# Decode attention with a gated MLP on one core: 16 instead of 24 rows of the output projection take the wide path, in steps of 4, and their sums are added earlier

## Chip, cores and metric

One core of one Trainium2 chip. The metric is the device time of one execution in microseconds (us). A "span" is the length of an execution inside the profile. It is shorter than the timed value of the same execution by 1.3 to 1.5 us in most executions and by 1.7 to 2.0 us in some, so that a time can be 0.5 us longer for a reason that lies outside the span.

In the profile PE is TensorE (its matmuls), PEld its loading of weights, PEq its sequencer, ACT ScalarE, DVE VectorE, POOL GpSimd and SP SyncE, which issues the loads. "Landing" is the signal that a load is complete. In a chain of waits, "issue" is time in which the engine waited for nothing that the profile shows. L716 is line 716 of the kernel.

## The reference, cut to what matters

```python
# one query token, 32 heads, 16384 cached keys and values, Dh = 128, D = 512
q = (x @ wq).reshape(1, 1, 32, 128).transpose(0, 2, 1, 3)
p = softmax(einsum('bhqd,bhkd->bhqk', q, k_cache) * Dh ** -0.5)
o = einsum('bhqk,bhkd->bhqd', p, v_cache)
a = o.transpose(0, 2, 1, 3).reshape(1, 1, 4096) @ wo        # wo: 4096 x 512, 4 MB
b = gated_mlp(x)                                            # small, done at the start
return g * a + (1 - g) * b
```

The caches are 2 x 128 MB, and every byte is read once. `wo` is the last thing read.

Of the kernel before, what the change touches and what calls it, by code (L numbers as in the profile page):

```python
# [31 lines left out]
NS = Dh // W  # L32
NG = KP // 4
TG = 8
WG = 8
NT = NG // TG
ZB = F // 4
K_CUTS = (0, 128, 256)
V_CUTS = (0, 160, 224, 256)
WO_CUTS = (0, 16, 24, 28, 31, 32)  # L40
WIDE = 24
inv_sqrt_dh = float(Dh) ** -0.5


# [39 lines left out]
def take(eng, sem, n=1):  # L84

    eng.wait_ge(sem, n).then_inc(sem, -n)  # L86


def matmul_again(nc, eng, out, lhsT, rhs, **flags):

    ins = eng.matmul(out, lhsT=lhsT, rhs=rhs, **flags).ins  # L91
    again = dataclasses.replace(ins, ldweights=False)
    todo = nc.cur_bb.bb.instructions
    assert todo[-1].name == ins.name
    todo[-1] = again
    return bass.BassInstruction(again)


def matmul_at(nc, eng, bank, col, shape, lhsT, rhs, static, again=False):


    m, n = shape
    flags = dict(start=False, stop=False, skip_group_check=True)
    with nc.discard():
        like = eng.matmul(bank[col:col + m, 0:n], lhsT=static[0], rhs=static[1], **flags).ins
    ins = eng.matmul(bank[0:m, 0:n], lhsT=lhsT, rhs=rhs, **flags).ins  # L106
    assert like.tile_size == ins.tile_size and like.tile_position == (0, col)
    moved = dataclasses.replace(ins, outs=like.outs, tile_position=like.tile_position,
                                ldweights=False if again else ins.ldweights)
    todo = nc.cur_bb.bb.instructions  # L110
    assert todo[-1].name == ins.name
    todo[-1] = moved
    return bass.BassInstruction(moved)


def matmul_on(nc, eng, emit, at, known={}):


    todo = nc.cur_bb.bb.instructions
    n = len(todo)  # L120
    ins = emit().ins
    new = list(todo[n:])
    assert new[-1].name == ins.name
    moving = [a for a in ins.ins if isinstance(a, mybir.RegisterAccessPattern)]
    assert len(moving) == len(at)
    ends = {a.regref: r for a, r in zip(moving, at)}
    set_here = {x.outs[0].regref for x in new[:-1]}
    for name in set(ends) - set_here:
        assert known[name] == ends.pop(name)
    live = {a.regref for a in ins.outs if isinstance(a, mybir.RegisterAccessPattern)}  # L130
    keep = [new[-1]]
    for x in reversed(new[:-1]):
        name = x.outs[0].regref
        if name in ends:
            reg, off = known[name] = ends.pop(name)
            assert isinstance(x, mybir.InstRegisterAlu) and x.op == ALU.add
            src, imm = x.ins
            imm = dataclasses.replace(imm, value=imm.value + off)
            x = dataclasses.replace(x, ins=(dataclasses.replace(src, regref=reg.name), imm))
        elif name in live:  # L140
            live |= {a.regref for a in x.ins if isinstance(a, mybir.RegisterAccess)}
        else:
            continue
        keep.append(x)
    assert not ends
    todo[n:] = keep[::-1]
    return bass.BassInstruction(new[-1])


def registers_first(nc, n, then=None):  # L150

    todo = nc.cur_bb.bb.instructions
    new = list(todo[n:])
    todo[n:] = [i for i in new if isinstance(i, mybir.InstRegisterAlu)]
    if then is not None:
        then()
    for i in new:
        if not isinstance(i, mybir.InstRegisterAlu):
            todo.append(i)
# [17 lines left out]
def gated_mix_kernel(nc, A_x, A_k_cache, A_v_cache, A_wq, A_wo, B_x, B_w_in, B_w_sp, B_b_sp,  # L177
# [83 lines left out]
    def counter(e, name, value):  # L261
        reg = e.alloc_register(name)
        e.reg_mov(reg, value)
        return reg
# [205 lines left out]
    def warm(e, n):  # L470
        for j in range(n):
            args = (m_ps[0], ident[:, :], zero[:, :])
            flags = dict(start=True, stop=True, skip_group_check=True)
            if j:
                matmul_again(nc, e, *args, **flags)
            else:
                e.matmul(args[0], lhsT=args[1], rhs=args[2], **flags)

    def fill(e, m, n=1):
        for _ in range(n):  # L480
            matmul_again(nc, e, m_ps[0][96:96 + m, :], ident[:, 0:m], zero[:, :], start=True,
                         stop=True, skip_group_check=True)
# [163 lines left out]
    def hand(e, loaded, to, n):  # L646
        e.wait_ge(loaded, 16).then_inc(to, n)
        e.nop().then_inc(loaded, -16)
# [34 lines left out]
    def pool_wo(e):  # L683
        e.wait_ge(*d_zero)
        e.wait_ge(*o2_ok)
        for j, (a, b) in enumerate(zip(WO_CUTS[:-1], WO_CUTS[1:])):
            if a < WIDE:
                hand(e, ld_o[j], wo_s, (min(b, WIDE) - a) // WG)

    pool.raw(pool_wo)  # L690

    def pe_wide(e):
        va, pa = (counter(e, n, 0) for n in ("wa", "oa"))
        warm(e, 2)
        with e.Fori(0, WIDE // WG) as t:
            w8 = wo[:, bass.ds(t * (WG * D), WG * D)]
            o8 = o2[:, bass.ds(t * WG, WG)]
            n = len(nc.cur_bb.bb.instructions)
            for j in range(WG):
                ins = matmul_on(nc, e, lambda: matmul_at(  # L700
                    nc, e, d_ps, 32 * (j % 4), (1, D), o8[:, j:j + 1], w8[:, j * D:(j + 1) * D],
                    (o2[:, 0:1], wo[:, 0:D])), [(va, in_wo + 2 * j * D), (pa, 2 * j)])
            registers_first(nc, n, lambda: take(e, wo_s))
            ins.then_inc(pe.sem, 1)
            fill(e, 1)
            e.reg_alu(va, va, 2 * WG * D, ALU.add)
            e.reg_alu(pa, pa, 2 * WG, ALU.add)

    pe.raw(pe_wide)
    pe.n += WIDE // WG  # L710
    w_ok = act.op(lambda e: e.copy(out=d_sb[:, :], in_=d_ps), wait=[(pe.sem, pe.n)], mark=True)


    def add(lhsT, rhs, wait, mark=False):
        for s in range(NC):
            ok = pe.op(lambda e, s=s: e.matmul(  # L716
                a_ps[32 * s:32 * s + 1, 0:DQ], lhsT=lhsT, rhs=rhs[:, s * DQ:(s + 1) * DQ],
                start=False, stop=False, skip_group_check=True), wait=wait if s == 0 else (),
                mark=mark and s == NC - 1, inc=(half, 1) if mark and s == 0 else None)
        return ok  # L720

    for j, (a, b) in enumerate(zip(WO_CUTS[:-1], WO_CUTS[1:])):
        for k in range(max(a, WIDE), b):
            y_ok = add(o2[:, k:k + 1], wo[:, k * D:(k + 1) * D],
                       [(ld_o[j], 16)] if k == a else (), k == H - 1)
        if b == 28:
            add(ones_f[:, 0:1], d_sb[:, :], [w_ok])
    for q in (dve, act):
        mine = range(NC)[:NC // 2] if q is dve else range(NC)[NC // 2:]
# [27 lines left out]
def build(inputs):  # L757
    import numpy as _np
    import concourse.bacc as _bacc
    from concourse import mybir as _mybir  # L760

    nc = _bacc.Bacc("TRN2", target_bir_lowering=False, num_devices=1, dynamic_dma_scratch_size=4096)
    arrays, args = {}, []
    for name in _INS:
        a = _np.ascontiguousarray(inputs[name])
        if a.dtype.kind in "iu":
            a = a.astype(_np.int64)
        arrays[f"in_{name}_dram"] = a
        args.append(nc.dram_tensor(f"in_{name}_dram", a.shape, _mybir.dt.from_np(a.dtype), kind="ExternalInput").ap())
    for i, (shape, dtype) in enumerate(_OUTS):  # L770
        dt = _mybir.dt.from_np(_np.dtype(dtype))
        args.append(nc.dram_tensor(f"out_{i}_dram", shape, dt, kind="ExternalOutput").ap())
    gated_mix_kernel(nc, *args)
    return nc, arrays
# [9 lines left out]
```

## The kernel before: what the change and the argument touch

Each of the 128 partitions holds 32 of the 4096 rows of `wo`; row k means the k-th of them, a 128 x 512 slice. The load of `wo` is split into five pieces, which land one after another (at 643.12, 645.61, 646.88, 647.87 and 648.15 us). The vector `o2` (128 x 32) holds the attention output, one column for each row.

A row can be multiplied in two ways. The *wide* way is one matmul of 512 columns into one of four strips of 32 array columns, so that four rows run side by side (in the first step below their matmuls start at 643.334 to 643.344 us and take 0.38 us each); it leaves four partial sums in the PSUM bank `d_ps`, which ACT copies to `d_sb` and a matmul with ones adds into `a_ps`. The *direct* way is two matmuls of 256 columns, in two strips, straight into `a_ps`.

```python
WG = 8                               # wide rows in one loop step
WO_CUTS = (0, 16, 24, 28, 31, 32)    # pieces of the load of wo, in rows
WIDE = 24                            # rows 0-23 go the wide way

def pool_wo(e):                      # POOL passes "piece has landed" on to PE, one unit for each step
    e.wait_ge(*d_zero); e.wait_ge(*o2_ok)
    for j, (a, b) in enumerate(zip(WO_CUTS[:-1], WO_CUTS[1:])):
        if a < WIDE:
            hand(e, ld_o[j], wo_s, (min(b, WIDE) - a) // WG)

def pe_wide(e):
    warm(e, 2)                       # matmuls on zeros, while PE waits
    with e.Fori(0, WIDE // WG) as t:
        ...                          # WG matmuls of 512 columns into strips j % 4 of d_ps;
        registers_first(nc, n, lambda: take(e, wo_s))     # before them, take one unit
        ins.then_inc(pe.sem, 1)
        fill(e, 1)                   # one matmul on zeros
        ...
w_ok = act.op(lambda e: e.copy(out=d_sb[:, :], in_=d_ps), wait=[(pe.sem, pe.n)], mark=True)

for j, (a, b) in enumerate(zip(WO_CUTS[:-1], WO_CUTS[1:])):
    for k in range(max(a, WIDE), b): # direct rows; the first of a piece waits for its landing
        y_ok = add(o2[:, k:k + 1], wo[:, k * D:(k + 1) * D],
                   [(ld_o[j], 16)] if k == a else (), k == H - 1)
    if b == 28:                      # the wide part's sums: between rows 27 and 28
        add(ones_f[:, 0:1], d_sb[:, :], [w_ok])
# then half of a_ps is copied to res by DVE, half by ACT (L731), and SP stores res
```

The softmax here doesn't subtract the row's maximum and nothing guards it: scores larger than these inputs give would overflow.

## Time and profile before

| | before |
|---|---|
| time, median of the first 3 runs | 651.94 us (651.72 to 652.34) |
| span of the profiled run | 650.2 us |
| bytes read, mean rate | 279.58 MB, 430 GB/s |
| PE busy, DVE busy | 65%, 52% |

From the page of the kernel before (part 1: busy us, share and count of instructions; part 2: busy tenths in 40 equal slices of the span):

```profile
span 650.2 us, 7735 instructions
...
PE 423.0 (65%) x2464; PEld 44.4 (7%) x1304; DVE 336.0 (52%) x159; ACT 45.8 (7%) x112; POOL 2.1 (0%) x10
...
PEclk9959788969779696987969798686978968798999
DMA  9999989999999999999999989999999999999898
...
HBM read 279.58 MB, written 0.00 MB: 430 GB/s over the span
```

The DMA engines are full from end to end (8 or 9 tenths busy in every slice), and no compute engine is (PE, the busiest, 65%). PEclk is the granted PE clock in tenths; it moves between slices (5 to 9 tenths), and it is high in the last ones (9 tenths in the last three).

The chain of waits of the kernel before, its last pieces (start us, us, what):

```profile
619.38 27.50 DMA bufs<-in_A_wo_dram
646.88 0.04 issue
646.92 1.64 PE ps_all L716 x20
648.56 0.02 issue
648.58 0.41 DVE res L731
```

The execution ends on the load of `wo`, the direct matmuls (L716) and one copy. The timeline of the same tail (start us, us, engine, line, operation, count, and in brackets the idle time before it and what ended it; L106 on `o` are the wide rows, L91 the filler, L716 on `d_sb` the sums):

```profile
643.33 0.60 PE L106 MATMUL ps_all<-bufs,o 128*1 x8 [0.54 <-PEq L86]
...
644.24 0.60 PE L106 MATMUL ps_all<-bufs,o 128*1 x8
...
645.80 0.60 PE L106 MATMUL ps_all<-bufs,o 128*1 x8 [0.73 <-PEq L86]
...
646.45 0.59 ACT L711 COPY d_sb<-ps_all 128x512 f32<-128x512 f32 x1 [6.02 <-PE ps_all L106]
...
646.92 0.60 PE L716 MATMUL ps_all<-bufs,o 128*1 128x256 bf16 x8 [0.31 <-DMA bufs<-in_A_wo_dram]
...
647.36 0.60 PE L716 MATMUL ps_all<-d_sb,const-float32-1.0 128*1 128x256 f32 x4
647.91 0.37 PEld L716 LDWEIGHTS ps_all<-bufs,o 128*1 128x1 bf16 x8 [0.47 <-DMA bufs<-in_A_wo_dram]
647.91 0.60 PE L716 MATMUL ps_all<-bufs,o 128*1 128x256 bf16 x8
```

PE waits three times for a piece of `wo`: before the third wide step (0.73 us idle), before row 24 (0.31) and before row 28. The last wait hides in the bracket of PEld, because the profile counts a matmul as busy for longer than its distance from the next (0.38 us for one of the sums, whose pairs start 0.21 us apart). From starts alone: the last pair of the sums started at 647.57 and fills 0.21 us, row 28 starts at 647.91, so PE had about 0.12 us to spare there.

### The profile page before, as it was taken

To read this page: it belongs to the slowest core of one execution; us is meant where nothing else is said; L and a number is where in the kernel's file an instruction comes from. 1 tells how busy PE (TensorE), PEld (TensorE's weight loads), DVE (VectorE), ACT (ScalarE), POOL (GpSimd) and SP (SyncE) were. 2 spreads that over 40 slices of the span, in tenths; PEclk is the share of its full clock that TensorE was granted. 3 is DMA by queue.
4 is the path that set the end of the run, shared out by engine and by line. 5 is a ranking of instruction groups with operands and counts; after the bars stand their busy time and mean duration, and the time that the engine had idled before them with its cause. 6 is when DMAs were issued, how large, how long until landed. Compare 5 with 4: busy or idle time off the path is not lost. (4 is left out here: it accounts for less than half of the span.)

```text
span 650.2 us, 7735 instructions
## 1 busy us (share of the span) xinstructions
PE 423.0 (65%) x2464; PEld 44.4 (7%) x1304; DVE 336.0 (52%) x159; ACT 45.8 (7%) x112; POOL 2.1 (0%) x10
## 2 busy tenths in 40 slices
PE   0547587847387574747857476584747757478767
PEld 0000000000101000010000101000010100001012
DVE  3457848256380845618265370835629075465600
ACT  2200100000001000010100001000010100001011
POOL 1000000000000000000000000000000000000000
PEclk9959788969779696987969798686978968798999
DMA  9999989999999999999999989999999999999898
GB/s 385 462 419 452 452 387 452 452 439 399 452 452 399 439 452 448 391 452 452 407 431 452 452 387 452 452 423 415 452 452 391 448 452 448 391 431 472 390 432 341
DMA packets 6203, 279.60 MB, mean 430 GB/s; under 512 B 695, under 2 KB 826, under 8 KB 1210
## 3 DMA queue, kind: packets, MB, share of 16 engines
q1 hardware_dynamic: 6194, 279.58, 99.6%
q8 instruction: 1, 0.02, 0.0%
q10 hardware_dynamic: 8, 0.00, 0.0%
HBM read 279.58 MB, written 0.00 MB: 430 GB/s over the span
## 5 line engine op out<-in xcount | busy, mean ns | idle before, releaser
L579 DVE TENSOR_TENSOR bufs<-bufs,qb x64 | 281.5, 4419 | 170.8 <-DVEq L86 170.8
L91 PE MATMUL ps_all<-bufs,ident 128*128 x960 | 261.6, 427 | 0.0
L496 PE MATMUL ps_all<-bufs,ident 128*128 x64 | 28.4, 444 | 153.8 <-PEq L86 153.8
L106 PE MATMUL ps_all<-bufs,p_t 128*8 x1024 | 79.2, 385 | 30.7 <-PEq L86 20.1
L564 DVE TENSOR_REDUCE s_sb<-ps_all 128x64 f32<-128x512 f32 x64 | 44.1, 688 | 95.0 <-DVEq L86 95.0
L91 PE MATMUL ps_all<-zero,ident 128*8 128x512 bf16 (+1 forms) x165 | 58.0, 383 | 0.0
L592 ACT ACTIVATE p_t<-s_sb 64x256 f32 (+1 forms) x32 | 13.3, 414 | 433.4 <-ACTq L86 433.0
L496 PEld LDWEIGHTS ps_all<-bufs,ident 128*128 128x128 bf16 x64 | 6.3, 99 | 367.7 <-issue 367.7
L106 PEld LDWEIGHTS ps_all<-bufs,p_t 128*8 x1024 | 17.9, 82 | 163.7 <-issue 163.5
L531 PE MATMUL ps_all<-pick,d_sb 128*128 128x2 f32 x128 | 16.9, 254 | 16.5 <-PEq L86 16.5
L531 PEld LDWEIGHTS ps_all<-pick,d_sb 128*128 128x128 f32 x128 | 15.7, 192 | 34.7 <-issue 34.7
L601 ACT COPY d_sb<-ps_all 128x512 f32<-128x512 f32 x16 | 9.4, 586 | 104.5 <-ACTq L86 104.5
L606 ACT CAST ps_all<-zero 128x512 f32<-128x512 bf16 x15 | 8.8, 589 | 1.7
L666 DVE RECIPROCAL rl<-ps_all 128x32 f32<-128x32 f32 x1 | 0.4, 357 | 11.3 <-PE ps_all L552 11.3
L669 DVE TENSOR_TENSOR o_sb<-ps_all,rl 128x32 bf16<-128x32 f32 x1 | 0.2, 192 | 11.5 <-PE ps_all L531 11.5
L592 ACT ACTIVATION_READ_ACCUMULATOR p_t<-s_sb (+1 forms) x32 | 5.9, 185 | 0.0
L381 DVE TENSOR_TENSOR bufs<-ps_all,ident 128x896 f32<-128x896 f32 x2 | 2.1, 1086 | 7.3 <-PE ps_all L91 7.3
L321 PE MATMUL ps_all<-xgw,const-float32-1.0 1*128 1x3 f32 x2 | 0.6, 360 | 8.0 <-DVE xgw L317 8.0
L106 PE MATMUL ps_all<-bufs,u 128*1 x14 | 2.6, 372 | 3.3 <-ACT ps_all L427 2.5
L91 PE MATMUL ps_all<-bufs,xb 128*128 x12 | 4.1, 467 | 0.0
L345 PE MATMUL ps_all<-bufs,xb 128*128 x4 | 1.9, 485 | 3.1 <-DMA bufs<-in_B_w_in_dram 3.1
L297 PE MATMUL ps_all<-const-bfloat16-1.0,x_row 1*128 1x128 bf16 x4 | 0.6, 302 | 4.8 <-DMA x_row<-in_A_x_dram 4.8
(76 smaller groups left out, 41.2 us busy)
## 6 DMA issues: line engine op xcount, KB each, us to landing
bufs<-in_A_k_cache_dram SPq DMA_DIRECT2D x2, 4096.0 KB, 35.7
bufs<-in_A_v_cache_dram SPq DMA_DIRECT2D x1, 5120.0 KB, 34.0
bufs<-in_A_wq_dram SPq DMA_DIRECT2D x1, 4096.0 KB, 12.3
bufs<-in_A_v_cache_dram SPq DMA_DIRECT2D x1, 2048.0 KB, 38.6
bufs<-in_A_wo_dram SPq DMA_DIRECT2D x1, 2048.0 KB, 24.6
bufs<-in_B_w_in_dram SPq DMA_DIRECT2D x1, 1792.0 KB, 15.5
bufs<-in_A_v_cache_dram SPq DMA_DIRECT2D x1, 1024.0 KB, 40.6
bufs<-in_A_wo_dram SPq DMA_DIRECT2D x1, 1024.0 KB, 26.7
```

The lines of the kernel that those rows point to most:

```text
L91: ins = eng.matmul(out, lhsT=lhsT, rhs=rhs, **flags).ins
L106: ins = eng.matmul(bank[0:m, 0:n], lhsT=lhsT, rhs=rhs, **flags).ins
L297: x_ok = pe.op(lambda e, c=c: e.matmul(m_ps[1][:, c * P:(c + 1) * P], lhsT=x_row[0:1, c::DC], rhs=ones_row[0:1, :], start=True, stop=True) ...
L345: if n else matmul_on(nc, e, lambda: e.matmul(args[0], lhsT=args[1], rhs=args[2], **flags), [at, (xa, 0)]))
L381: dve.op(lambda e, h=h, zh=zh: e.tensor_tensor(out=zm[:, 2 * h * ZB:2 * (h + 1) * ZB].rearrange("p (b m k) -> p b m k", b=2, k=FhC), in0=z ...
L496: matmul_on(nc, e, lambda: e.matmul(s3, lhsT=ident[:, :], rhs=k3[:, :, 0:W], start=True, **flags), [(kw, 0)])
L531: ins = e.matmul(o2, lhsT=d_sb[:, r * Dh:(r + 1) * Dh], rhs=pick[:, r * 2:(r + 1) * 2], start=False, stop=False, skip_group_check=True)
L564: return e.tensor_reduce(out=s_sb[:, c * QK:(c + 1) * QK], in_=s_ps[c % 2].rearrange("p (j w) -> p j w", w=W), axis=AX.X, op=ALU.add)
L579: e.tensor_tensor(out=k3, in0=k3, in1=qi, op=ALU.mult).then_inc(mul_s, 1)
L592: e.activation(out=p_t[rows, bass.ds(at, NG * 8)].rearrange("p (t c) -> p t c", c=8)[:, :, 4 * s:4 * s + 4], in_=s_sb[rows, :].rearrange(" ...
L601: return e.copy(out=d_sb[:, :], in_=d_ps)
L606: e.copy(out=d_ps, in_=zero[:, :]).then_inc(drn_s, 1)
```

## The change

Intent: shorter wide steps, fewer wide rows, and the wide part's sums out of the stretch just before the last loads land.

```diff
-WG = 8
+WG = 4
-WIDE = 24
+WIDE = 16
...
     def pe_wide(e):
-        warm(e, 2)
+        warm(e, 3)
...
-        if b == 28:
+        if b == 24:
             add(ones_f[:, 0:1], d_sb[:, :], [w_ok])
```

Rows 16 to 23 move from the wide to the direct way (16 matmuls of 256 columns more, 8 of 512 fewer), the wide rows 0 to 15 go in four steps of 4 and not in two of 8, the sums follow row 23, and PE does one warm-up matmul more. POOL no longer passes on the piece of rows 16 to 23, which PE now waits for itself. No load changes.

## The prediction

> **What bounds the kernel now.** The loads do. The page's DMA row is 9 tenths in nearly all slices, at a mean of 430 GB/s for 279.6 MB over a span of 650.2 us; PE is busy 65%, DVE 52%. [...] The change touches only the output projection, whose weights are the last loads, so only what follows the last landings can change the time.
>
> The chain of waits ends: load of wo until 646.88, direct matmuls (L716) until 648.56, copy (L731) 0.41 us. In the trace the five pieces of wo land at 643.12 (rows 0-15), 645.61 (16-23), 646.88 (24-27), 647.87 (28-30) and 648.15 us (31). The timeline shows PE waiting for each: wide steps start at 643.30, 644.21 and, after 0.73 us idle, 645.77; rows 24-27 at 646.92; the sums of the wide part at 647.36 to about 647.79; rows 28-30 at 647.91, after a wait for their load; row 31 from 648.2. So the end is the last two landings plus about 2.0 us of matmul, copy and store. PE's slack before row 28 is only about 0.12 us.
>
> **What the change does.** No load changes, and PE's instructions are the same up to the tail.
> - One warm-up matmul more, about 0.21 us start to start. It ends near 642.85, before the first landing (643.12): free.
> - Wide loop: 4 steps of 4 instead of 2 of 8. A step of 8 took 0.91 us (643.30 to 644.21), though its matmuls and filler need only 0.65: PE's sequencer bounds it (semaphore, three register operations at 0.133 us, a branch of 0.2). With two register operations I estimate 0.76 us per step. The last begins at about 645.6; its sums are out at 646.0, 1.2 us later than row 15 before, but there PE was idle.
> - Rows 16-23 go direct, without the hop over POOL: 8 x 0.109 us (start to start of pairs in L716) = 0.87 us, from about 646.05 to 646.9.
> - ACT's copy of the wide sums (0.59 us) runs about 646.05 to 646.65 (before: 646.45 to 647.04), hidden behind the direct rows. The fp32 sum matmuls (4 x 0.107 us) run 646.9 to 647.35.
> - Rows 24-27 (landed 646.88): 647.35 to 647.8. Rows 28-30 wait for 647.87, as before; row 31 follows.
>
> So work moves within PE's slack before the last two landings, and PE is again idle about 0.1 us before row 28. Gain: none, the last landing rules. Loss: none, or up to 0.2 us if my step estimate is short.
>
> **Prediction.** 651.9 us, range 651.2 to 652.7 (before: 651.72 to 652.34). Faster by over 2%: 0.5%; within 2%: 98.5%; slower by over 2%: 1%.
>
> **What would show it.** Right: bytes and DMA row unchanged; row 28 still waits for its load and begins 0.04 us after it; the copy L731 starts about 0.4 us after the last landing; wide steps 0.7 to 0.8 us apart; ACT's L711 at about 646.05; sum matmuls without a wait on ACT. Wrong in a step: wide steps 0.91 us apart, so that PE reaches row 28 after its landing.
>
> **What would make it wrong.** A throttled PE clock in the tail (the page shows slices at 0.6 elsewhere) doubles 1.7 us of matmuls: over 1 us longer, still 0.2%. Loads that run at another rate move the time more than this change can.

## The result, and the profile after

| | before | after |
|---|---|---|
| time, median of 6 runs | 651.78 us (651.63 to 652.34) | 651.65 us (651.50 to 651.82) |
| ratio | | 0.9997, 95% interval 0.9984 to 1.001 |
| span | 650.2 us | 650.2 us |
| first wide step to ACT's copy of the sums | 643.33 to 646.45 | 643.34 to 646.09 |
| last piece of `wo` lands | 648.15 | 648.19 |
| last matmul starts | 648.24 | 648.27 |

A ratio is the mean time of one kernel's runs over that of the other's of the same rounds, so it is not quite the ratio of the medians. In e10 below the changed kernel, unaltered, gave 651.72 against 651.67.

The page of the changed kernel:

```profile
span 650.2 us, 7753 instructions
...
PE 424.3 (65%) x2474; PEld 47.0 (7%) x1312; DVE 335.8 (52%) x159; ACT 45.8 (7%) x112; POOL 2.2 (0%) x10
...
PEclk9959798958889796888969679796977969698979
DMA  9999999999999999999999999999999999999998
...
HBM read 279.58 MB, written 0.00 MB: 430 GB/s over the span
```

The same bytes at the same rate. Its chain of waits, the last pieces:

```profile
619.02 28.88 DMA bufs<-in_A_wo_dram
647.89 0.04 issue
647.94 0.65 PE ps_all L716 x8
648.58 0.02 issue
648.61 0.41 DVE res L731
```

The chain now leaves the loads one piece later (rows 28 to 30, landed 647.89, and not rows 24 to 27): PE no longer waits for the piece in between. Behind it stand the matmuls of rows 28 to 31 and the same copy. The timeline of the tail:

```profile
643.34 0.39 PE L106 MATMUL ps_all<-bufs,o 128*1 x4 [0.28 <-PEq L86]
...
644.11 0.39 PE L106 MATMUL ps_all<-bufs,o 128*1 x4 [0.16 <-PEq L86]
...
644.86 0.39 PE L106 MATMUL ps_all<-bufs,o 128*1 x4
...
645.65 0.39 PE L106 MATMUL ps_all<-bufs,o 128*1 x4 [0.19 <-PEq L86]
645.88 0.38 PE L91 MATMUL ps_all<-zero,ident 128*1 128x512 bf16 x1
...
645.93 1.04 PE L716 MATMUL ps_all<-bufs,o 128*1 128x256 bf16 x16
646.09 0.59 ACT L711 COPY d_sb<-ps_all 128x512 f32<-128x512 f32 x1 [5.61 <-PE ps_all L106]
...
646.80 0.60 PE L716 MATMUL ps_all<-d_sb,const-float32-1.0 128*1 128x256 f32 x4
...
647.23 1.31 PE L716 MATMUL ps_all<-bufs,o 128*1 128x256 bf16 x16
647.94 0.38 PEld L716 LDWEIGHTS ps_all<-bufs,o 128*1 128x1 bf16 x8 [0.40 <-DMA bufs<-in_A_wo_dram]
```

Between the landing of rows 0 to 15 and row 28 PE now waits for no load: the wide steps, the direct rows 16 to 23, the sums and rows 24 to 27 follow each other. Only before row 28 does it wait, 0.40 us in PEld's bracket. The last pair of row 27 starts at 647.56 and takes 0.11, so 0.27 us of that is idle array.

So the change filled PE's waits and moved its work, and left the last landing and what follows it as they were.

### The profile page after: what moved, and what is told of

Read it like the earlier page. It is cut to its first block, busy times and chain, and to the rows that moved or that the text cites. A ratio compares the mean times of both kernels' runs of the same rounds, so it can differ in the third digit from the quotient of the medians.

```text
span 650.2 us, 7753 instructions
## 1 busy us (share of the span) xinstructions
PE 424.3 (65%) x2474; PEld 47.0 (7%) x1312; DVE 335.8 (52%) x159; ACT 45.8 (7%) x112; POOL 2.2 (0%) x10
## 3 DMA queue, kind: packets, MB, share of 16 engines
q1 hardware_dynamic: 6194, 279.58, 99.6%
HBM read 279.58 MB, written 0.00 MB: 430 GB/s over the span
## 5 line engine op out<-in xcount | busy, mean ns | idle before, releaser
L91 PE MATMUL ps_all<-bufs,ident 128*128 x960 | 258.8, 423 | 0.0
L106 PE MATMUL ps_all<-bufs,p_t 128*8 x1024 | 82.5, 396 | 30.1 <-PEq L86 20.1
L91 PE MATMUL ps_all<-zero,ident 128*8 128x512 bf16 (+2 forms) x167 | 59.5, 388 | 0.0
L106 PEld LDWEIGHTS ps_all<-bufs,p_t 128*8 x1024 | 19.4, 83 | 163.1 <-issue 161.6
L91 PE MATMUL ps_all<-bufs,xb 128*128 x12 | 5.0, 552 | 0.0
L106 PE MATMUL ps_all<-bufs,xb 128*64 x32 | 3.6, 380 | 0.0
```

The source lines that it names most:

```text
L91: ins = eng.matmul(out, lhsT=lhsT, rhs=rhs, **flags).ins
L106: ins = eng.matmul(bank[0:m, 0:n], lhsT=lhsT, rhs=rhs, **flags).ins
```

## The experiments

Theory A: the end is the last two landings plus a fixed piece of work, and PE's tail is slack of 0.1 to 0.3 us. Theory B, the rival: PE's total work in the tail is what counts, and the two forms happen to cost the same. All runs below took part in 5 rounds against the kernel before. The record marks the result of every run correct, and that of the two short loads too, although these multiply rows 28 to 31 by the wrong weights; the mark therefore says little about the last rows.

| run | edit | time us | before | ratio (95%) | median span | last landing | last matmul starts |
|---|---|---|---|---|---|---|---|
| e10 | changed kernel again | 651.72 | 651.67 | 1.0001 (0.9987 to 1.0015) | 650.3 | 648.35 | 648.40 |
| e1 | sums after row 31 | 652.31 | 651.66 | 1.0006 (0.9992 to 1.002) | 650.5 | 648.40 | 648.80 |
| e2 | 10 fillers before row 28 | 654.05 | 651.66 | 1.0033 (1.0019 to 1.0047) | 652.3 | 648.63 | 650.80 |
| e3 | all rows direct | 652.85 | 651.66 | 1.0012 (0.9998 to 1.0025) | 651.5 | 649.44 | 649.64 |
| e4 | last 8 rows in one load | 652.73 | 651.66 | 1.001 (0.9996 to 1.0023) | 650.8 | 648.18 | 648.99 |
| e5 | wide steps of 8 | 651.79 | 651.67 | 1.0001 (0.9987 to 1.0015) | 650.4 | 648.72 | 648.77 |
| e6 | only the sums moved | 651.76 | 651.67 | 1.0001 (0.9987 to 1.0015) | 650.2 | 648.17 | 648.29 |
| e7 | no filler, no warm-up | 652.71 | 651.67 | 1.0015 (1.0001 to 1.0029) | 651.3 | 648.50 | 649.42 |
| e8 | last two loads left out | 651.72 | 651.81 | 0.9998 (0.9984 to 1.0012) | 649.9 | 646.91 | 648.04 |
| e9 | the same, all rows direct | 651.04 | 651.81 | 0.9992 (0.9978 to 1.0005) | 649.7 | 647.17 | 647.98 |
| e11 | 40 empty instructions on PE | 652.96 | 651.98 | 1.0014 (1.0001 to 1.0028) | 651.4 | 648.93 | 648.98 |
| e12 | all rows direct, rows 0-15 in a loop | 651.63 | 651.98 | 0.9995 (0.9981 to 1.0009) | 650.3 | 648.23 | 648.32 |

Nine of the twelve intervals hold 1, so the times alone carry little. The median span of the five executions (650.2 us for the changed kernel's first six; 650.2 to 650.5 for the kernel before) leaves out what lies outside the span, and the two right-hand columns, each from one profile, are what a step of 0.2 to 1 us can be read from. The landing is the latest of the 16 DMA engines' signals for the last piece.

### The changed kernel again (e10)

> The changed kernel unaltered, as the reference on this chip for the three beside it. Both theories: 651.65 us, ratio to before 0.9995 to 1.0005.

Measured: 651.72 us against 651.67, with a spread of 651.55 to 652.40. It fixes the noise: single executions of either kernel lie up to 1.0 us above the median of their call (the largest: 652.62 against 651.66, the kernel before in the call of e1).

### Sums after the last row (e1)

```diff
-        if b == 24:
-            add(ones_f[:, 0:1], d_sb[:, :], [w_ok])
+    y_ok = add(ones_f[:, 0:1], d_sb[:, :], [w_ok], True)      # after the loop over the pieces
```

> The changed kernel with the sums of the wide part added after row 31 and no longer between rows 23 and 24. Theory (the last landing plus the PE work after it is the end): 0.43 us more work now lies behind the last landing (two fp32 passes 0.213 us apart, a matmul 0.107 us longer), so the last matmul starts at about 648.69 and not 648.26, and the time is 0.4 us over the changed kernel's, 652.05. Rival (only the total of PE's work in the tail counts, which two forms happen to share): same work, same time, 651.65.

Measured: the last matmul starts 0.40 us after the last landing, against 0.08 in the changed kernel. The time is 652.31, a little over what A expects and away from B's 651.65, but its interval holds 1, so it is the profile that decides. The place of the sums costs when they lie behind the last landing. e6 shows the other half of it.

### Ten fillers before row 28 (e2)

```diff
+        if a == 28:
+            pe.raw(lambda e: warm(e, 10))
```

> The changed kernel with ten more filler matmuls (2.15 us at full clock) ahead of row 28. Theory: PE has 0.27 us of idle there, so about 1.9 us of it shows at the end: last matmul at about 650.15, time 653.5. Rival (the end is set by the loads alone and PE has ample slack in the tail): under 0.3 us more. It also shows that a change of 2 us in the tail can be seen in the times at all.

Measured: 654.05 us, so 2 us of PE work are not swallowed: the variant of the rival with ample slack is out. It is 0.5 us over A's figure. In the profiled execution (span 652.7) one DMA engine had been 0.44 us late since about 100 us, so even rows 0 to 15 landed at 643.57 and not 643.13, and with PE as the bound everything behind that landing moves. The other four spans, 652.2 to 652.4, are 2.0 to 2.2 us over the changed kernel's, where A had said 1.9; the rest of their excess lies outside the span (three of the four have the larger difference).

### Only the wide steps, and only the sums (e5, e6)

```diff
-WG = 4                     # e5, on the changed kernel
+WG = 8
-        if b == 28:        # e6, on the kernel before
+        if b == 24:
```

> The changed kernel with wide steps of 8 again: 2 steps and not 4 for the 16 wide rows. Theory: a step takes 0.91 us, the second ends about 0.7 us before the fourth step of 4 did, PE idles until rows 16-23 land (645.62) and these start at about 645.66 and not 645.93; PE idles 0.27 us more before row 28 and the time is unchanged, 651.65. Rival (PE's work in the tail is on the path): 0.3 us faster.

> The kernel before (24 wide rows in steps of 8) with only the sums moved between rows 23 and 24. Theory: the sums wait for ACT's copy until 647.04, go 647.1 to 647.5, rows 24-27 after them until about 647.95, so PE's slack before row 28 is used up: row 28 starts 0.0 to 0.1 us late, time within 0.1 us of before. PE then waits for ACT and not for the load of rows 24-27. Rival (the place of the sums was what the change gained or lost by): the same ratio to before as the changed kernel has, whatever that is.

Measured: both within 0.12 us of the kernel before. In e5 the profiled run also had a DMA engine 0.46 us late, so its landings can't be set against the others; its two wide steps lie 0.91 us apart as expected (643.89 and 644.80), and row 28 waits for its load from about 647.95 to 648.44. In e6 the sums do wait for ACT, as expected. The timeline of e6:

```profile
646.46 0.58 ACT L711 COPY d_sb<-ps_all 128x512 f32<-128x512 f32 x1 [6.02 <-PE ps_all L106]
647.09 0.09 PEld L716 LDWEIGHTS ps_all<-d_sb,const-float32-1.0 128*1 128x1 f32 x4 [1.19 <-ACT d_sb L711]
647.09 0.60 PE L716 MATMUL ps_all<-d_sb,const-float32-1.0 128*1 128x256 f32 x4 [0.47 <-ACT d_sb L711]
...
647.52 1.04 PE L716 MATMUL ps_all<-bufs,o 128*1 128x256 bf16 x16
```

All 16 matmuls of rows 24 to 31 follow without a gap, so the slack before row 28 is used up to nothing, and the last matmul starts 0.12 us after the last landing, against 0.09 before. Moving the sums alone would have left no reserve; it is fewer wide rows that let ACT's copy start at 646.09 and made room.

### One load for the last eight rows (e4)

```diff
-WO_CUTS = (0, 16, 24, 28, 31, 32)
+WO_CUTS = (0, 16, 24, 32)
```

> The changed kernel with rows 24-31 of the weights in one load and not three. Theory: all eight rows wait for the last landing (about 648.19), so the last row's matmul starts 7 x 0.109 us later than the first one's at 648.24, at 649.0 and not 648.26: 0.74 us over the changed kernel, 652.4. Rival (bytes loaded set the time): same bytes, same time, or less by the issues saved.

Measured: the last landing is the same (648.18), the last matmul starts 0.81 us after it, against 0.08. All five spans are 650.8 or 650.9, 0.6 to 0.7 us longer (expected: 0.74); the median time is 652.73, 0.3 over what was expected, because three of the five executions have the larger difference between time and span. The work behind the last landing is what counts, not the bytes, which are equal.

### Without the last two loads (e8, e9)

```diff
+        if a < 28:          # rows 28-31 are not loaded; they use row 27's weights (wrong result)
             sp.op(lambda e, a=a, b=b: e.dma_start(out=wo[:, a * D:b * D], ...
```

> The changed kernel without the last two loads (rows 28-31; they are computed with row 27's weights, so the result is wrong on purpose). The last landing is then that of rows 24-27, at about 646.9 and not 648.19, 1.28 us earlier. If loads alone ruled: 1.28 us faster, 650.4. Theory (PE has only 0.27 us of slack before row 28): PE, now not waiting, sets the end; its last matmul starts at about 648.0 and not 648.26: 0.27 us faster, 651.4.

> The same two loads left out (wrong result on purpose), with all 32 rows direct. Theory: PE waits for rows 24-27 (646.9) and then does eight rows in 0.87 us, last matmul at about 647.71 and not 648.26: 0.55 us faster than the changed kernel, 651.1, and 0.3 us faster than the short load with the wide rows. If loads alone ruled: 1.28 us, 650.4, in both.

Measured: with the wide rows the last landing comes 1.28 us earlier, but the last matmul only 0.23 us earlier (648.04 and not 648.27). The chain of waits of e8:

```profile
645.69 0.39 PE ps_all L106 x4
646.08 0.16 PE ps_all L91
646.24 2.12 PE ps_all L717 x35
648.36 0.02 issue
648.38 0.41 DVE res L732
```

There is no wait for a load in it: PE is the bound, from the last wide step on. This is the size of the reserve: the changed kernel sits 0.2 to 0.3 us below the point where PE takes over. The time, 651.72, missed the expected 651.4; the spans did not (649.8 to 650.0, so 0.2 to 0.4 us under the changed kernel's 650.2, where 0.27 was expected), and three of the five executions have the larger difference. With all rows direct (e9) PE waits for the last piece again (647.17), and the time is 0.6 us under the changed kernel's, the median span 0.5, as expected. Its one profile does not show that gain in full (last matmul at 647.98 and not the expected 647.71), as there the last piece landed 0.26 us later than in e8. The theory that the loads alone rule would have had 1.28 us in both; it is wrong by about 1 us for e8. A holds with its second half: the last landing rules, with little to spare.

### No filler and no warm-up (e7)

```diff
-    pe.raw(lambda e: warm(e, 2))     # and warm(e, 1), warm(e, 3), fill(e, 1) in the output projection
```

> The changed kernel without warm-up and filler matmuls in the output projection. Two outcomes: if the clock that is granted falls to half there, the matmuls behind the wide loop double (direct rows 0.218 us each, sums 0.85), PE reaches row 28 late, and the time is 1 to 2 us longer (652.6 to 653.7); if it stays at full, nothing changes (651.65), as the fillers lie in slack. My theory of the end takes either; I hold the second a bit more likely[...].

Measured: 652.71 us, 1.0 us over the changed kernel, the first of the two outcomes and not the one held more likely. Two windows of the changed kernel and of this one (busy us of each engine with counts, granted clock, DMA share, GB/s):

```profile
641.60:645.00 3.40, 2.50 (x22) 0.71 (x19) 0.40 (x2) 0.00 (x0) 0.00 (x0) 1.00 0.98 408
645.00:648.40 3.40, 3.11 (x46) 1.51 (x40) 0.00 (x0) 0.59 (x1) 0.00 (x0) 1.00 0.73 281
```

```profile
641.60:645.00 3.40, 1.75 (x13) 0.51 (x13) 0.44 (x3) 0.00 (x0) 0.00 (x0) 0.50 0.94 395
645.00:648.40 3.40, 3.09 (x29) 1.49 (x28) 0.00 (x0) 0.58 (x1) 0.00 (x0) 0.50 0.84 323
```

The granted clock is 1.00 in the changed kernel's trace and 0.50 in this one. The pairs of rows 16 to 23 lie 0.213 us apart and not 0.109, PE reaches row 28 after its landing (648.19), and the last matmul starts 1.15 us later (0.31 of that is this run's later landings: the last is at 648.50 and not 648.19). The half clock is no peculiarity of this run: the clock records of the kernels before and after hold only 1.00 and 0.50, each for 3.41 us or a multiple of it (but for the last record), and matmuls of 512 columns (L91 on `bufs`) start 0.216 us apart at the one and 0.427 us apart at the other. In e7 the half clock held from 641.6 to 648.4, two windows of 3.4 us, and the clock was 1.00 again after it; in the second of them PE was busy for 3.09 us. In the window before the fall, from 638.2 to 641.6, PE was busy for 2.30 us of 3.40 (changed kernel: 3.04, and its clock stayed at 1.00). What makes the clock fall and return is not shown. A lower clock in the tail is the one danger that the prediction had named, and it is real.

The fillers do not rule it out. In the profiles of e4 and e6, which have them, the clock was also 0.50, from 641.1 to 644.4. In e4, whose wide loop is the changed kernel's, the warm-up matmuls then ran past the first landing (643.23), the first wide step started at 644.36 and not 643.34, and the sums at 647.01 and not 646.80. That 0.21 us would have left the changed kernel 0.06 us of its 0.27; in e4 it is hidden behind the later landing of rows 24 to 31.

### All rows direct, and what made it slow (e3, e11, e12)

```diff
-WIDE = 16
+WIDE = 0       # e3: no wide loop, no copy of sums, no sum matmuls; row 0 waits for o2 itself
```

> All 32 rows direct: no wide loop, no copy of sums by ACT, no sum matmuls. Theory: rows 0-15 take 16 x 0.109 = 1.75 us from the first landing (643.13) and end at about 645.0, before rows 16-23 land (645.62); PE then waits for each landing, 0.5 us idle before row 28, and the time is that of the changed kernel within 0.1 us, 651.65. Rival (PE's work in the tail is on the path): the wide loop's 2.6 us and the sums' 0.43 us are gone against 1.75 us of direct rows, so 0.5 to 1.3 us faster.

Measured: 652.85 us (652.16 to 652.93), over the changed kernel by 1.1 to 1.2 us (651.72 in e10, 651.65 at first). Neither A's 651.65 nor B's gain. The timeline of e3:

```profile
643.36 1.91 PE L713 MATMUL ps_all<-bufs,o 128*1 128x256 bf16 x32 [0.15 <-DMA bufs<-in_A_wo_dram]
...
647.13 0.60 PE L713 MATMUL ps_all<-bufs,o 128*1 128x256 bf16 x8 [0.24 <-DMA bufs<-in_A_wo_dram]
649.31 0.31 PEld L713 LDWEIGHTS ps_all<-bufs,o 128*1 128x1 bf16 x8 [1.88 <-DMA bufs<-in_A_wo_dram]
649.31 0.60 PE L713 MATMUL ps_all<-bufs,o 128*1 128x256 bf16 x8 [1.58 <-DMA bufs<-in_A_wo_dram]
```

PE did its part as expected, with rows 0 to 15 done by 645.1, and then stood idle for 1.58 us before row 28. The loads came late, not the matmuls. The signals of the single DMA engines and the packets in the trace show why (us from the start of the span; part 3 of the page lists the instruction packet, as one packet of queue q8):

```
                                    before    after     e3        e12       e11
rows 28-30, 15 of 16 engines done   647.67    647.81    648.06    647.90    648.23
rows 28-30, the 16th                647.87    647.89    649.27    647.94    648.61
row 31,     15 of 16 engines done   648.08    648.10    648.38    648.20    648.54
row 31,     the 16th                648.15    648.19    649.44    648.23    648.93
instruction packet, 16 KB, from     647.51    647.32    647.11    647.35    647.43
                            took      1.08      1.10      1.08      1.10      1.10
```

Every one of the 14 profiles has exactly one such 16 KB packet near the end, 1.06 to 1.33 us long. In e3 the last eight 1 KB packets of `wo` start at 648.18, when it has ended (648.19), and take 0.06 to 0.14 us each and not 0.046; all the other 120 had started by 647.89. So one DMA engine served the instruction packet ahead of its share of the last pieces (the trace does not name the DMA engines; eight packets of 128 are one engine's share). In the other profiles the last pieces were not held up by it (in the four listed beside e3 the 16th engine comes 0.03 to 0.39 us after the 15th). The packet's start tells them apart: in e3 it lies 0.69 us before the first DMA engine's signal for the last piece, in the other 13 profiles at most 0.48 us before it. The last signal comes about 0.5 us after the start of the last packet of `wo` (647.66 and 648.15 before, 647.70 and 648.19 after), so by this reckoning, an estimate, only in e3 was no DMA engine done with its loads when the instruction packet started. In e3 the 16th engine came 1.21 us after the others for rows 28 to 30 and 1.06 us for row 31, and the last landing is 1.25 us later than the changed kernel's.

That gave a new theory, a guess which nothing up to here shows: the longer PE's program, the sooner the packet comes. It starts at 647.11 in e3 (299 PE instructions by my count of the built program), at 647.32 in the changed kernel (259; 647.70 in its other profile, e10) and at 647.51 before (235). Two runs were made for it; from what was expected of e11 a clause on what sets the packet off is cut, as no run shows it.

```diff
+    for _ in range(40):                                   # e11, at the start of PE's program
+        pe.raw(lambda e: e.nop().then_inc(pad_s, 1))
-    one wide matmul of 512 columns into d_ps per row      # e12, in the loop of 4 steps
+    two direct matmuls of 256 columns into a_ps per row, no filler, no sums
```

> The changed kernel with 40 empty semaphore instructions (on a semaphore of their own) at the very start of PE's program, where PE waits for x anyway; the tail's work is untouched. New theory of why the all-direct kernel was 1.1 us slower: each trace has one 16 KB instruction load near the end (1.08 us on one DMA engine); [...] 40 more instructions ahead bring it forward, as the longer unrolled program of the all-direct kernel did; it then goes ahead of that DMA engine's packets of the last weights. So: the instruction load starts before 647.2 (647.32 and 647.70 in the two profiles of the changed kernel), one DMA engine lands the last pieces about 1 us after the other 15, and the time is 652.4 to 653.0. Rival (it is the direct rows themselves, or their unrolling, that cost): 651.65, as the tail is the same.

> All 32 rows direct, as in the all-direct run, but rows 0-15 in a loop of 4 steps of 4 rows, so that PE's program is as long as the changed kernel's (258 against 259 instructions, 299 in the all-direct run). No copy of sums, no sum matmuls, no filler in the loop. New theory (the instruction load, not the direct rows, cost 1.1 us): steps of about 0.76 us, rows 0-15 done by about 646.2, the instruction load at 647.3 or later behind the last packets, all 16 DMA engines land within 0.5 us, time 651.65. Rival (direct rows for all 32 cost by themselves): 652.7 as in the all-direct run.

e12 came out as expected: all 32 rows direct, 258 PE instructions, 651.63 us, all DMA engines within 0.53 us of each other on the last piece, and PE waits for row 28 again:

```profile
646.24 1.48 PE L715 MATMUL ps_all<-bufs,o 128*1 128x256 bf16 x24
647.99 0.37 PEld L715 LDWEIGHTS ps_all<-bufs,o 128*1 128x1 bf16 x8 [0.56 <-DMA bufs<-in_A_wo_dram]
647.99 0.60 PE L715 MATMUL ps_all<-bufs,o 128*1 128x256 bf16 x8 [0.27 <-DMA bufs<-in_A_wo_dram]
```

So direct rows cost nothing by themselves; of the rival to the new theory only the unrolling is left. e9 speaks against that too: it has e3's unrolled rows, without the last two loads, and was not slow. Its packet came earliest of all (646.52, against 647.05 in e8 with the shorter program), as the theory would have it, and still held up nothing. e11 reached the time that was expected (652.96, all five runs over 652.8) but not by the way that was expected: in its one profile the instruction packet starts at 647.43 and holds nothing up; instead two DMA engines had been 0.2 and 0.6 us behind the third-latest since about 100 us, so rows 0 to 15 landed at 643.89 and the last row at 648.93; the wide steps, 0.92, 0.85 and 0.77 us apart, were slower than the changed kernel's too, and the chain of waits ends on PE, whose last matmul (648.98) came just as its load did. Its other four spans (651.4 to 651.7) are longer still, and have no profile. e11 therefore confirms nothing. What is shown: in the profiled run of e3 the instruction packet held one DMA engine while the last weights waited on it. What is open: which engine the packet is for, what decides when it is asked for, whether the length of PE's program moves it, whether the unprofiled runs of e3 were slow for the same reason, and why e11 was slow.

No version beat both kernels clear of noise: e12 is equal (651.63), and it needs neither the sums, nor ACT's copy of them, nor the filler in the loop.

## Why the prediction was right, point by point

- **The bound.** "The loads do." Shown: 651.65 us, within 0.3 us of the forecast 651.9 and well inside 651.2 to 652.7; the bytes (279.58 MB), the rate (430 GB/s) and the last landing (648.15 and 648.19) are unchanged. e4 and e1 show that work moved behind that landing adds to the time, e2 and e7 that work ahead of it does so too once it exceeds the slack.
- **The warm-up matmul is free.** The last of the three starts at 642.69 in the trace and fills 0.21 us, before the first landing (643.13). In e4, at a granted clock of 0.50, it was not: the warm-up matmuls ran past the first landing (643.23).
- **Wide steps of 0.76 us, bound by PE's sequencer.** Measured start to start: 0.77, 0.75 and 0.79 us (the sequencer's part is at the end of this text). The last starts at 645.65 (forecast: about 645.6); ACT's copy starts at 646.09 (forecast: 646.05).
- **Rows 16 to 23 in 0.87 us.** Measured: 645.93 to 646.80, 0.87 us. They started 0.12 us sooner than forecast. The estimate had them wait for the last filler; the trace has them start 0.05 us after it. Why was not shown.
- **Sums without a wait on ACT.** ACT was done at 646.67, the sums started at 646.80.
- **Row 28 waits for its load, 0.04 us after the landing.** Measured: 647.89 and 647.94; the copy L731 started 0.42 us after the last landing (forecast: about 0.4).
- **"PE is again idle about 0.1 us before row 28."** Mis-sized: 0.27 us. Rows 16 to 23, and with them all that follows, came 0.12 us sooner than forecast. It errs on the harmless side; e8 confirmed the size by making PE the bound (0.23 us gained of 1.28).
- **"A throttled PE clock in the tail ... over 1 us longer."** Tried in e7: 1.0 us in the time, 1.15 us in the last matmul (0.84 from the last landing on: 0.92 us behind it and not 0.08).
- **What it did not see.** An instruction packet of 1.1 us shares the DMA engines with the last loads. It did no harm here, but e3 shows that it can do as much (1.2 us of landing) as the clock. The change makes PE's program 24 instructions longer; that this moves the packet is not shown.

The gain that one might have hoped for went into slack: 0.15 us more of idle PE before row 28, where idle time is worth nothing. It would be worth something as a reserve, as for a lower clock in the wide loop (0.21 us in e4); that it ever saved time is not shown. Whether the spread of times is narrower for it can't be told: 651.50 to 651.82 in the first six runs, 651.55 to 652.40 in the next five.

## What to carry to other kernels

Where a kernel is full of loads to the end, write down when each of the last pieces lands and when the compute that uses it starts; a change of the tail can gain only what lies behind the last landing, and can lose as soon as the compute reaches it late, which here was 0.1 to 0.3 us away. Keep matmuls on zeros in such a tail if the array would idle: without them, in e7, it ran at half its clock (0.50 from 641.6 to 648.4) and the time grew by 1.0 us. They do not guarantee the full clock (0.50 from 641.1 to 644.4 in e4 and e6). And when a variant with less work is slower, look at the landings of the single DMA engines before blaming its instructions.

## What else the traces show

- In the wide loop of the changed kernel the compare-and-branch took 201 to 209 ns when taken and 69 ns when it fell through, and the loop step of 0.76 us was bound by it and the register operations around it: from the first branch to the next step's first weight load 0.58 us passed (643.50 to 644.08), in which PE's sequencer ran these and one semaphore instruction.
- In 3 of 14 profiles (e2, e5, e11) a DMA engine, in e11 two, fell behind the others between the landings at 96 and 116 us, and stayed behind to the end, 530 us later. At the landing of rows 0 to 15 the latest engine was 0.44 us (e2) and 0.46 us (e5) after the next one, in e11 the last two 0.24 and 0.64 us after the third-latest. It is part of the noise of this load-bound kernel.
